# Loading gate and up weights from two DMA queues, and half of a filter from the Pool queue, in a spectral + GEGLU block

## Chip, cores and metric

One core of one Trainium2 chip. The metric is the device time of one execution in microseconds (us); where several executions were timed, the median is given with the lowest and highest. "Span" is the profiled time from the first to the last instruction, some 2 us shorter than the device time.

TensorE is PE, VectorE DVE, ScalarE ACT, GpSimd POOL, SyncE SP. In this kernel PE, DVE and ACT compute (ACT also issues one table load), SP only issues DMAs, and POOL does both.

## The reference, cut to what matters

```python
x = A_x                                     # 2048 x 576, bf16
h = x + irfft2(rfft2(layernorm(x)) * (w_r + 1j * w_i))    # filter w: 2048 x 289, real and imaginary plane
n = layernorm(h)
out = h + (gelu(n @ w_gate) * (n @ w_up)) @ w_down         # w_gate, w_up: 576 x 4608, w_down: 4608 x 576
```

## The kernel before

The kernel has two parts. The spectral part does both FFTs as matmuls with tables: stage A (scaled tables x X), stage D/B (tables, filter multiply on DVE), stage I/N (inverse). The feed-forward part works on four blocks of 512 rows; for each it computes gate and up (K = 576 as 9 slices of 64 rows: gate on the upper 64 rows of the array, up on the lower 64), then the down projection.

A small scheduler (`Prog`) turns read and write keys into semaphore waits. Each engine executes its own list in order; `P.dma(ENGINE, ...)` puts a DMA into that engine's list and so on that engine's queue.

The loads, in the order in which SP issues them (`...` marks cuts):

```python
for i, (c0, c1) in enumerate(((0, 2), (2, 4), (4, 8), (8, 12), (12, 16))):
    P.dma(SP, XO[:, c0:c1, :], xv[:, c0:c1, :], f"x{i}", ...)            # X tiles
P.dma(ACT, ATB..., dram["ATAB"])                                         # the table that is scaled
P.dma(SP, FT ...); P.dma(SP, BT ...); P.dma(SP, VT ...)                  # tables
for hf, (g0, g1) in enumerate(((1, 9), (9, 16))):                        # filter: 36 small DMAs, rows of 578 B
    for pl, src in ((0, A_w_r), (1, A_w_i)):
        ...  P.dma(SP, WS[jj:64:4, g0:g1, pl, 0:K2], a, f"w{pl}{hf}", ...)
P.dma(SP, DT ...); P.dma(SP, IT ...); P.dma(SP, IDT ...)                 # tables of the inverse stage
```

The weights of the feed-forward part. Gate lies on partitions 0 to 63 of `WGU`, up on 64 to 127. `WD` shares its memory with the filter and the spectral data, so w_down must wait until the filter multiply is over (the `alias`):

```python
P.op(POOL, None, r=["IT", "DT"])            # Pool waits until IT and DT have landed
for j in range(9):
    f0, f1 = 512 * j, 512 * j + 512
    P.dma(POOL, WGU[0:64, :, f0:f1], wgv[:, :, f0:f1], f"wg{j}", w=[("WG", j, 0)])
    P.dma(POOL, WGU[64:128, :, f0:f1], wuv[:, :, f0:f1], f"wg{j}", w=[("WG", j, 1)])
P.alias(ukeys + wkeys[0] + wkeys[1] + [...], [("WD", j) for j in range(9)])
for j in range(9):
    P.dma(POOL, WD[:, 4 * j:4 * j + 4, :], wdv[:, 4 * j:4 * j + 4, :], f"wd{j}", w=[("WD", j)])
```

Block 0's activations are turned on PE while the inverse stage runs (tiles c = 0 to 3, at passes 7, 9, 11, 13 of 16), evicted to `HT0`, and then each half is copied to the other half of the partitions by two small SBUF-to-SBUF DMAs on SP's queue. These eight copies ("HT<-HT", 256 rows of 256 B each) are what the first gate/up matmul waits for:

```python
def turn_pe(c):
    ...                                                     # 5 matmuls with the identity, one DVE copy to HT0
    P.dma(SP, HT0[0:64, 5:9, t0:t1], HT0[64:128, 0:4, t0:t1], f"tr{c}", ...)
    P.dma(SP, HT0[64:128, 5:9, t0:t1], HT0[0:64, 1:5, t0:t1], f"tr{c}", ...)
for c in range(NT + 1):                                     # inverse stage
    ...
    if c in (6, 8, 10, 12): norm((c - 6) // 2)
    if c in (7, 9, 11, 13): turn_pe((c - 7) // 2)
```

## Time and profile before

| | before |
|---|---|
| device time, median of 3 | 535.7 us (535.35 to 536.09) |
| span of the profiled run | 534.1 us |
| PE busy | 508.4 us, 95% |
| first spectral matmul (FT,U) | 21.4 us |
| first gate load issued | 35.5 us |
| first gate/up matmul | 106.5 us |

PE at 95% looks like a kernel with nothing left. The chain of waits shows the rest. Its columns are start in us, length in us, and what it was: an engine with the tile and line it worked on, a DMA in flight, or an engine's sequencer ("SPq").

```profile
90.23 16.04 DMA HT_69<-HT_69
106.27 0.25 issue
106.52 4.03 PE PS L683 x18
...
115.38 64.41 PE PS L683 x593
```

One wait of 16 us stands between the spectral part and the feed-forward part, on the HT<-HT copies. After 115 us the chain is PE alone. (HT_69 is `HT0`, L683 the gate/up matmul.)

The DMA table gives, for each kind of DMA, how often, the size of one, and the median time from issue to landing: 16 us for a copy of 64 KB.

```profile
HT_69<-HT_69 SPq DMA_DIRECT2D x8, 64.0 KB, 16.0
```

The stretches of 10 us show why. Columns: stretch, its length, busy us (and instructions) of PE, PEld, DVE, ACT and POOL; then the granted clock, the busy share of the DMA engines, and GB/s.

```profile
core 0: us, PE busy (x) PEld busy (x) DVE busy (x) ACT busy (x) POOL busy (x), PEclk, DMA share, GB/s
0.00:10.00 10.00, 7.19 (x24) 2.71 (x24) 4.09 (x16) 5.24 (x14) 3.52 (x11) 1.00 0.82 312
10.00:20.00 10.00, 9.26 (x86) 6.32 (x87) 8.97 (x40) 9.20 (x23) 2.76 (x3) 0.83 0.91 244
20.00:30.00 10.00, 9.01 (x76) 6.29 (x74) 5.64 (x17) 4.92 (x11) 0.00 (x0) 1.00 0.43 92
30.00:40.00 10.00, 10.00 (x90) 7.19 (x89) 7.60 (x28) 6.18 (x13) 4.55 (x6) 1.00 0.66 195
40.00:50.00 10.00, 10.00 (x90) 7.17 (x88) 7.61 (x29) 6.18 (x13) 8.74 (x13) 1.00 1.03 216
...
90.00:100.00 10.00, 0.46 (x4) 0.15 (x2) 0.77 (x2) 2.00 (x5) 0.00 (x0) 0.69 1.05 339
```

From 40 us on the DMA engines are full (share 1.03), at 216 GB/s with gate and up and 339 GB/s with w_down. Between 20 and 30 us they are less than half busy: there SP issues filter loads one after another, and Pool waits. Pool's timeline (start, length, engine, line, operation, tiles, in brackets the idle time before it and what ended it):

```profile
14.98 1.04 POOL L419 TENSOR_TENSOR ATS<-ATB,RS_56 128x512 bf16<-128x512 bf16 x1 [1.66 <-DVE RS_56 L417]
35.45 0.92 POOL L193 DMA_DIRECT2D WGU<-in_B_w_gate_dram  x1 [19.43 <-DMA IT<-c_itab]
```

### The profile page before, as it was taken

What the parts mean: (1) busy time and instruction counts of PE and PEld (TensorE: products, weight loads), DVE (VectorE), ACT (ScalarE), POOL (GpSimd) and SP (SyncE); (2) the same over time, 40 slices, a digit from 0 to 9 for tenths busy, and PEclk for the clock granted to TensorE, in tenths of its full rate; (3) what the DMA queues carried; (4) which work ended last, traced back from release to release, by engine and by line L of the source; (5) the groups of instructions that cost most, each with busy time, mean ns of one, the idle gap of its engine ahead of it and who ended that gap; (6) DMA issues with size and microseconds to landing.
All of it is one profiled execution on the core that took longest, in us unless ns stands there. A gap on an engine that the chain in (4) does not pass through costs nothing.

```text
span 534.1 us, 10212 instructions
## 1 busy us (share of the span) xinstructions
PE 508.4 (95%) x4427; PEld 296.4 (55%) x4427; DVE 184.2 (34%) x428; ACT 152.8 (29%) x285; POOL 26.3 (5%) x40
## 2 busy tenths in 40 slices
PE   7999897099999999999999999999999999999997
PEld 3667575034444677444446774444477744444776
DVE  5677667033443211344332113433321133333111
ACT  6756587033243100233331002333210033223000
POOL 3036220000000000000000000000000000000000
PEclk9999999589999999999999999999999999999999
DMA  8669999801110000011100000111000000000000
GB/s 326 137 169 215 215 216 270 273 1 26 26 26 17 7 18 18 9 26 28 24 14 6 18 18 12 26 26 26 11 7 18 18 6 1 1 1 2 12 18 18
DMA packets 34684, 30.76 MB, mean 58 GB/s; under 512 B 21296, under 2 KB 29616, under 8 KB 34640
## 3 DMA queue, kind: packets, MB, share of 16 engines
q0 software_dynamic: 4176, 15.93, 12.5%
q1 hardware_dynamic: 30320, 13.66, 9.6%
q8 instruction: 35, 0.57, 0.5%
q10 hardware_dynamic: 144, 0.52, 0.3%
q14 instruction: 9, 0.07, 0.0%
HBM read 23.67 MB, written 2.36 MB: 49 GB/s over the span
## 4 chain that ended last, share of the span: by engine, by line
PE 91%; DMA 4%; DVE 3%; ACT 1%; issue 1%; POOL 0%; SPq 0%; DVEq 0%; POOLq 0%
PE PS L683 52%; PE PS L699 27%; PE PS L513 4%; DMA HT_69<-HT_69 3%; PE PS L590 3%; PE PS L527 1%; PE PS L546 1%; PE PS L435 1%; DMA XO<-in_A_x_dram 1%; PE PS L428 1%; DVE XO L602 1%; PE PS L550 1%; PE PS L599 1%; ACT JNK L392 0%; DVE HT_69 L648 0%
## 5 line engine op out<-in xcount | busy, mean ns | idle before, releaser
L690 ACT ACTIVATE GL<-PS 128x512 bf16<-128x512 f32 x144 | 85.8, 597 | 294.1 <-PE PS L683 286.7
L683 PE MATMUL PS<-HT_69,WGU 64*128 64x512 bf16 x1296 | 142.8, 380 | 16.2 <-DMA HT_69<-HT_69 16.1
L691 DVE TENSOR_TENSOR AT<-GL,PS 128x512 bf16<-128x512 bf16 x144 | 98.7, 687 | 167.4 <-ACT GL L690 167.2
L699 PE MATMUL PS<-WD,AT 128*128 128x288 bf16 x1152 | 141.8, 286 | 0.0
L683 PE MATMUL PS<-HT_84,WGU 64*128 64x512 bf16 x1296 | 140.2, 376 | 0.0
L699 PEld LDWEIGHTS PS<-WD,AT 128*128 128x128 bf16 x1152 | 112.4, 98 | 29.9 <-issue 1.7
L683 PEld LDWEIGHTS PS<-HT_69,WGU 64*128 64x128 bf16 x1296 | 63.4, 95 | 94.7 <-issue 18.7
L683 PEld LDWEIGHTS PS<-HT_84,WGU 64*128 64x128 bf16 x1296 | 62.9, 94 | 76.8 <-issue 0.5
L702 DVE TENSOR_TENSOR OS<-PS,XO 128x288 bf16<-128x288 f32 x32 | 14.7, 458 | 123.7 <-PE PS L699 123.7
L590 PE MATMUL PS<-DT,V 128*128 128x288 bf16 x160 | 22.1, 286 | 0.5 <-ACT V L553 0.5
L513 PE MATMUL PS<-FT,U 128*128 128x289 bf16 x160 | 22.3, 287 | 0.0
L602 DVE SCALAR_TENSOR_TENSOR XO<-PS,XO 128x576 bf16<-128x576 f32 x16 | 12.1, 757 | 27.9 <-PE PS L599 27.7
L590 PEld LDWEIGHTS PS<-DT,V 128*128 128x128 bf16 x160 | 15.4, 98 | 4.3 <-issue 0.6
L605 ACT ACTIVATE SQ<-XO 128x576 bf16<-128x576 bf16 x16 | 10.9, 683 | 23.2 <-DVE XO L602 23.0
L513 PEld LDWEIGHTS PS<-FT,U 128*128 128x128 bf16 x160 | 14.4, 97 | 5.1 <-issue 0.4
L428 PE MATMUL PS<-ZD 128*128 128x512 bf16 x39 | 12.0, 462 | 1.3 <-POOL ZD L356 1.3
L628 DVE TENSOR_SCALAR HN<-XO,TM,RS_59 128x576 bf16<-128x576 bf16 (+1 forms) x32 | 10.2, 361 | 8.0 <-DMA HT_84<-HN 6.2
L546 PE MATMUL PS<-VT,ZS 128*128 128x256 bf16 x64 | 9.6, 271 | 2.4 <-DVE ZS L537 1.6
L399 DVE BATCH_NORM_STATS2 ST_53<-XO 128x6 f32<-128x288 bf16 x24 | 9.2, 443 | 5.6 <-DMA XO<-in_A_x_dram 5.6
L532 DVE TENSOR_TENSOR T_79<-YS,WS 128x580 bf16<-128x580 bf16 x16 | 7.4, 460 | 10.4 <-ACT YS L530 10.4
L530 ACT ACTIVATE YS<-PS 128x578 bf16<-128x578 f32 x16 | 10.5, 656 | 1.5 <-PE PS L527 0.3
L592 ACT ACTIVATE GS<-PS 128x576 bf16<-128x576 f32 x16 | 10.2, 635 | 2.6 <-PE PS L590 2.6
(57 smaller groups left out, 170.8 us busy)
## 6 DMA issues: line engine op xcount, KB each, us to landing
WGU<-in_B_w_gate_dram POOLq DMA_DIRECT2D x9, 576.0 KB, 22.8
WGU<-in_B_w_up_dram POOLq DMA_DIRECT2D x9, 576.0 KB, 24.8
WD<-in_B_w_down_dram POOLq DMA_DIRECT2D x9, 576.0 KB, 31.6
out_dram<-OS SPq DMA_DIRECT2D x32, 72.0 KB, 1.6
XO<-in_A_x_dram SPq DMA_DIRECT2D x3, 576.0 KB, 6.9
HT_84<-HN SPq DMA_TRANSPOSE x72, 2.4
FT<-c_ftab SPq DMA_DIRECT2D x1, 725.0 KB, 8.9
DT<-c_dtab SPq DMA_DIRECT2D x1, 720.0 KB, 4.6
```

The costliest lines, as they stand in the source:

```text
L428: P.op(PE, lambda t: t.matmul(bank(7), ZD[:, 0:128], ZD[:, :], start=True, stop=True), r=["ZD"], w=[("PS", 7)])
L513: P.op(PE, lambda t, b=b, o=o, dt=dt, g=g: t.matmul(bank(b, 0, 128, 0, K2), U[:, dt, g, :, :], FT[:, dt, o, 0:K2], start=(dt == 0), stop=( ...
L530: P.op(ACT, lambda a, sl=sl: a.activation(YS[:, sl, :, 0:K2], banks(4, 2, K2), ACTF.Copy), r=[("PS", 4), ("PS", 5)], w=[("Y", sl)])
L546: P.op(PE, lambda t, c=c, zp=zp, sl=sl, sp_=sp_: t.matmul(bank(6, 0, 128, 256 * c, 256 * c + 256), ZS[:, sl, zp, 128 * c:128 * c + 128], V ...
L590: P.op(PE, lambda t, b=b, h=h, kt=kt, c=c: t.matmul(bank(b, 0, 128, 0, 288), V[:, kt, c, :, :], DT[:, kt, 288 * h:288 * h + 288], start=(k ...
L602: P.op(DVE, lambda v, x2=x2, c=c: v.scalar_tensor_tensor(x2, banks(4, 2, 288), 1.0, x2, op0=ALU.mult, op1=ALU.add, accum_out=SB2[:, 0, c:c ...
L605: P.op(ACT, lambda a, sl=sl, c=c: a.activation(SQ[:, sl, :], XO[:, c, :], ACTF.Square, accum_out=SB2[:, 1, c:c + 1]), r=[("X", c)], w=[("S ...
L683: P.op(PE, lambda t, o=o, h0=h0, kt=kt, sl=sl, f=f, b0=b0, HT=HT: t.matmul(bank(b0 + o), WGU[h0:h0 + 64, kt, 128 * f:128 * f + 128], HT[h0 ...
L690: P.op(ACT, lambda a, s2=s2, b0=b0: a.activation(GL[:, s2, :], bank(b0), ACTF.Gelu_apprx_tanh), r=[("PS", b0)], w=[("GL", s2)])
L691: P.op(DVE, lambda v, s2=s2, b0=b0, f=f: v.tensor_tensor(AT[:, f, :], GL[:, s2, :], bank(b0 + 1), op=ALU.mult), r=[("GL", s2), ("PS", b0 + ...
L699: P.op(PE, lambda t, b0=b0, h=h, f=f, p=p: t.matmul(bank(b0 + h, 0, 128, 0, 288), AT[:, f, 128 * p:128 * p + 128], WD[:, f, 288 * h:288 * ...
L702: P.op(DVE, lambda v, b0=b0, h=h, p=p, c=c: v.tensor_tensor(OS[:, p % 2, 288 * h:288 * h + 288], bank(b0 + h, 0, 128, 0, 288), XO[:, c, 28 ...
```

## The change

Its intent: start the weights earlier and load gate and up at the same time, so that the copies find free DMA engines. The imaginary filter plane moves from SP to Pool, in the gaps between Pool's table scalings; Pool no longer waits for IT and DT; the up weights go on SP's queue.

```diff
-    for hf, (g0, g1) in enumerate(((1, 9), (9, 16))):
-        for pl, src in ((0, A_w_r), (1, A_w_i)):
-            ... all 36 filter loads on SP
+    def w_loads(pl, hf, eng):
+        ... the same loads, returned as a list of calls that issue on eng
+    for f in w_loads(0, 0, SP) + w_loads(0, 1, SP):      # real plane
+        f()
 ...
+    for f in w_loads(1, 0, POOL):                        # imaginary plane, first half: 8 loads
+        f()
+    wrest = w_loads(1, 1, POOL)                          # second half: 10 loads
 ...
     ln1_scale(0, POOL)
+    for f in wrest[:4]: f()
 ...
     ln1_scale(1, POOL)
+    for f in wrest[4:7]: f()
 ...
     ln1_scale(2, POOL)
+    for f in wrest[7:]: f()
 ...
-    P.op(POOL, None, r=["IT", "DT"])
     for j in range(9):
         f0, f1 = 512 * j, 512 * j + 512
         P.dma(POOL, WGU[0:64, :, f0:f1], wgv[:, :, f0:f1], f"wg{j}", w=[("WG", j, 0)])
-        P.dma(POOL, WGU[64:128, :, f0:f1], wuv[:, :, f0:f1], f"wg{j}", w=[("WG", j, 1)])
+        P.dma(SP, WGU[64:128, :, f0:f1], wuv[:, :, f0:f1], f"wu{j}", w=[("WG", j, 1)])
```

More of the change, by code (lines that the diff above doesn't have):

```diff
@@ L367, in _build @@
     P.dma(SP, VT[:, :, :, :].rearrange("p a b c -> p (a b c)"), dram["VTAB"][:, :], "vt", w=["VT"])
-    for hf, (g0, g1) in enumerate(((1, 9), (9, 16))):
-        for pl, src in ((0, A_w_r), (1, A_w_i)):
-            for jj in range(4):
-                a = bass.AP(src.tensor, (16 * jj + g0) * K2, [[128 * K2, 16], [K2, g1 - g0], [1, K2]])
-                P.dma(SP, WS[jj:64:4, g0:g1, pl, 0:K2], a, f"w{pl}{hf}", r=["Wz"], w=[("W", hf, pl, jj)])
-                a = bass.AP(src.tensor, (64 + 16 * jj + 16 - g0) * K2, [[128 * K2, 16], [-K2, g1 - g0], [1, K2]])
-                P.dma(SP, WS[64 + jj:128:4, g0:g1, pl, 0:K2], a, f"w{pl}{hf}", r=["Wz"], w=[("W", hf, pl, 4 + jj)])
-            if hf:
-                for p0 in range(2):
-                    a = bass.AP(src.tensor, 64 * p0 * K2, [[128 * K2, 16], [16 * K2, 4], [1, K2]])
-                    P.dma(SP, WS[64 * p0:64 * p0 + 64, 0, pl, 0:K2], a, f"w{pl}{hf}", r=["Wz"], w=[("W", hf, pl, 8 + p0)])
+    def w_loads(pl, hf, eng):
+        g0, g1 = ((1, 9), (9, 16))[hf]
+        src = (A_w_r, A_w_i)[pl]
+        o = []
+        for jj in range(4):
+            o.append((WS[jj:64:4, g0:g1, pl, 0:K2], (16 * jj + g0) * K2, [[128 * K2, 16], [K2, g1 - g0], [1, K2]], jj))
+            o.append((WS[64 + jj:128:4, g0:g1, pl, 0:K2], (64 + 16 * jj + 16 - g0) * K2, [[128 * K2, 16], [-K2, g1 - g0], [1, K2]], 4 + jj))
+        if hf:
+            for p0 in range(2):
+                o.append((WS[64 * p0:64 * p0 + 64, 0, pl, 0:K2], 64 * p0 * K2, [[128 * K2, 16], [16 * K2, 4], [1, K2]], 8 + p0))
+        return [lambda d=d, off=off, ap=ap, h=h: P.dma(eng, d, bass.AP(src.tensor, off, ap), f"w{pl}{hf}", r=["Wz"], w=[("W", hf, pl, h)]) for d, off, ap, h in o]
+    for f in w_loads(0, 0, SP) + w_loads(0, 1, SP):
+        f()
     GORD = list(range(1, NG)) + [0]
@@ L459, in _build @@
     ln1_scale(0, POOL)
+    for f in wrest[:4]:
+        f()
     ln1_tile(5)
@@ L471, in _build @@
     ln1_scale(1, POOL)
+    for f in wrest[4:7]:
+        f()
     ln1_tile(9)
@@ L484, in _build @@
     ln1_scale(2, POOL)
+    for f in wrest[7:]:
+        f()
     ln1_tile(13)
```

## The prediction

> **What bounds the kernel now.** The feed-forward matmuls are 79% of the chain of waits and untouched: from 115.4 us to 531.5 us the chain is PE alone. What can move lies before. The chain's largest wait is one piece of 16.0 us (90.2 to 106.3): the small SBUF-to-SBUF copies HT<-HT, the turned activations of the first token block. Similar small transfers take 2.2 to 2.8 us (DMA table) when little else runs. These are slow because weights still stream: in the windows view the DMA engines are at 1.02 to 1.06 from 40 to 100 us, at 215 GB/s while gate and up chunks (64 partitions each) load, at 320 to 340 GB/s for w_down (128 partitions). The first gate load is issued only at 35.5 us: the timeline shows Pool idle for 19.4 us, waiting for IT. In the stall the granted clock falls to 0.5, and the first 18 gate/up matmuls take 4.03 us instead of 1.95.
>
> **What changes.** (a) The IT/DT wait goes. SP issues 18 fewer filter loads (0.64 us each) and reaches the up weights at about 18.6 us; Pool reaches the gate weights at about 21 to 22. Gate and up are 10.6 MB: at the old 215 GB/s they end by about 71 us. w_down cannot start before the filter multiply ends (63.4 before, about 66 after) and needs about 17 us: all ends by 84 to 88 us. The Trainium skill, "SBUF — State Buffer", section "Door 1: The DMA port swizzle", gives 64 partitions 8 of 16 ports, about 218 GB/s; the trace's 215 agrees. Its next section says that two DMAs to the two halves gain only 6%; I don't need more, and expect 220 to 300 GB/s. So the last HT copy, issued at about 92 us, meets empty queues: 2.3 us instead of 16.
>
> (b) The cost: Pool now issues 18 filter loads around the table scalings, which are on the chain (POOL ATS, 9.65 to 10.7). Estimate: 0.73 us each, as Pool's weight loads take in the timeline. Eight from 4.05 us end near 10.0, four and three more follow: the third scaling, ended at 16.0 before, ends at 18.7 to 19.7. The early filter packets also interleave with the X tiles, which now arrive just in time (ACT is not idle before tile 7). The spectral stage, starting at 21.4, should start 2 to 3.5 us later.
>
> **Sum.** First gate/up matmul: now 106.5; after 92.3 + 3 = 95.3, a gain of about 11 us. PE is then idle for some 2 us only, so the clock probably stays at 1.0: another 2 us. Total about 12.7 us: 523 us, range 519.5 to 527.5. Faster by over 2% (under 525.0): 0.70; within 2%: 0.29; slower: 0.01.
>
> **What would show each step.** HT<-HT on the chain under 4 us; first gate load issued at 20 to 23 us; first gate/up matmul at 94 to 97 us; first spectral matmul (FT,U) at 23 to 25 us; Pool's issues between scalings 0.6 to 0.9 us each; at most one 3.4 us stretch of clock 0.5 near 92 to 98 us; the part from 115.4 us to the end as long as before.
>
> **What would make it wrong.** Pool's issues cost over 1 us, so the spectral stage slips by 5 us or more (527 to 529); X tiles are starved by filter packets; the up loads, in 1 KB packets against Pool's 4 KB, finish so late that they hold up the HT copies behind them; or the short idle still drops the clock (+2 us). If Pool's issues are cheaper (0.4 us), the result is near 520.

## The result, and the profile after

| | before | after |
|---|---|---|
| device time, median | 535.89 us (535.35 to 537.4, 4 runs) | 528.5 us (526.48 to 529.1, 4 runs) |
| span of the profiled run | 534.1 us | 526.9 us |
| first spectral matmul (FT,U) | 21.37 us | 21.61 us |
| first gate load issued | 35.5 us | 17.9 us |
| last HT<-HT copy landed | 106.3 us | 98.45 us |
| first gate/up matmul | 106.52 us | 98.81 us |
| from there to the end of the span | 427.6 us | 428.1 us |

The ratio is 0.9851, 95% interval 0.9818 to 0.9884. (A ratio is the mean time of one kernel's fast runs over that of the other's of the same rounds, so not quite the ratio of the medians.) The change gains 1.5%, less than the 2% that counts as a verdict, and 528.5 lies above the predicted range.

The chain of waits after:

```profile
88.71 0.74 DVE HT_69 L659
...
91.31 2.04 SPq L193
...
94.94 3.51 DMA HT_69<-HT_69
98.45 0.35 issue
98.81 4.02 PE PS L694 x18
```

The DMA piece shrank from 16.0 to 3.5 us, but that isn't the whole wait. The last tile's DVE copy ended at 89.2 us before and 89.45 us after, and its second HT<-HT copy, which was issued at 90.2 us before, is issued at 94.94 us now. SP could not issue it sooner. The wait has moved in part from "DMA" to "SPq". The DMA table agrees: issue to landing of a copy is now 7.4 us, not 16.0.

```profile
HT_69<-HT_69 SPq DMA_DIRECT2D x8, 64.0 KB, 7.4
```

SP's own timeline suggests that its queue was full (inferred from the times to issue; the trace has no fill level). The nine up loads took SP 51 us to issue, the eight copies 17.8 us (by themselves about 0.6 us each):

```profile
21.27 51.13 SPq L193 DMA_DIRECT2D WGU<-in_B_w_up_dram  x9
78.49 17.82 SPq L193 DMA_DIRECT2D HT_69<-HT_69  x8
```

The stretches of 10 us after (four left out, with 200 to 304 GB/s and a share of 1.05 to 1.13; columns as before):

```profile
0.00:10.00 10.00, 7.43 (x24) 2.77 (x24) 4.20 (x16) 4.53 (x11) 7.88 (x19) 1.00 0.83 292
10.00:20.00 10.00, 7.79 (x81) 4.96 (x83) 8.72 (x39) 9.66 (x25) 9.97 (x16) 1.00 1.07 267
20.00:30.00 10.00, 8.81 (x77) 6.29 (x76) 5.88 (x18) 4.99 (x11) 4.49 (x7) 1.00 1.10 221
30.00:40.00 10.00, 10.00 (x90) 7.19 (x88) 7.35 (x28) 6.18 (x13) 0.00 (x0) 1.00 1.03 209
...
80.00:90.00 10.00, 9.91 (x88) 7.48 (x86) 8.91 (x27) 8.27 (x20) 0.00 (x0) 1.00 1.05 318
90.00:100.00 10.00, 1.89 (x12) 0.78 (x12) 0.98 (x5) 2.09 (x5) 0.00 (x0) 0.72 0.79 155
```

The DMA engines are now busy from 10 us until the copies have landed (a share of 1.03 to 1.13 up to 90 us, 0.93 from there to 98.45 us). The column GB/s times 10 us can be added up. Up to 20 us 5.6 MB have moved in both kernels (before 312 + 244, after 292 + 267). Up to the first gate/up matmul 24.3 MB move in both. So after 20 us 18.7 MB are still to come, whoever issues them. The change filled the idle of the stretch 20 to 40 us; it removed no bytes.

Which queue got what comes from the DMA records of the trace, here for 72 to 88 us after the change. A packet is one such record. The means include the records of a few bytes that end a DMA:

| queue | packets | mean size | mean time of one | rate |
|---|---|---|---|---|
| Pool's (w_down) | 992 | 4.1 KB | 211 ns | 254 GB/s |
| SP's (the last up loads) | 993 | 1.0 KB | 56 ns | 62 GB/s |

The packet counts are equal: the queues take turns, packet by packet. Pool's packets hold four rows (4.1 KB of gate, 4.6 KB of w_down), SP's a single row. The rows of gate and up are equally long (1 KB each), so the difference is how the rows went into packets on the two queues. The filter shows it too: its rows of 578 B went in packets of one row on SP's queue and of up to eight rows (4.6 KB) on Pool's. The Trainium skill, "DMA: Bandwidth & Descriptors", section "Queues, rings and completion order", says that each DMA engine goes round between its queues packet by packet, and the counts 992 and 993 agree. With turns of 4 to 1 KB, the up loads crawl at 62 GB/s while w_down streams. The last two up chunks landed at 94.4 and 96.8 us, and the copies stood behind them in SP's queue.

Pool's side of the change went better than I had expected:

```profile
3.94 4.31 POOL L193 DMA_DIRECT2D WS<-in_A_w_i_dram  x8
9.55 1.03 POOL L425 TENSOR_TENSOR ATS<-ATB,RS_56 128x512 bf16<-128x512 bf16 x1 [1.30 <-issue]
10.53 2.16 POOL L193 DMA_DIRECT2D WS<-in_A_w_i_dram  x4
...
15.33 1.05 POOL L425 TENSOR_TENSOR ATS<-ATB,RS_56 128x512 bf16<-128x512 bf16 x1
17.91 6.59 POOL L193 DMA_DIRECT2D WGU<-in_B_w_gate_dram  x9
```

A filter load (128 rows) takes Pool 0.54 us to issue (4.31 / 8), not the 0.73 us of a weight load (576 rows; 6.59 / 9). The issues mostly fit between the scalings, the third of which starts 0.35 us later than before. The spectral stage starts 0.24 us later.

### The profile page after: what moved, and what is told of

Its sections match the earlier page's. It is cut to its first block, busy times and chain, and to the rows that moved or that the text cites. A ratio compares the mean times of both kernels' runs of the same rounds, so it can differ in the third digit from the quotient of the medians.

```text
span 526.9 us, 10210 instructions
## 1 busy us (share of the span) xinstructions
PE 507.8 (96%) x4425; PEld 302.5 (57%) x4427; DVE 184.1 (35%) x428; ACT 152.8 (29%) x285; POOL 29.1 (6%) x49
## 4 chain that ended last, share of the span: by engine, by line
PE 88%; SPq 3%; DVE 3%; DMA 3%; ACT 2%; issue 1%; DVEq 0%; ACTq 0%
PE PS L694 51%; PE PS L710 27%; PE PS L525 4%; PE PS L601 3%; SPq L191 2%; DMA XO<-in_A_x_dram 2%; PE PS L539 1%; SPq L193 1%; PE PS L558 1%; ACT U L453 1%; DMA HT_69<-HT_69 1%; PE PS L610 1%; PE PS L562 1%; DVE XO L613 1%; DMA HT_84<-HN 0%
## 5 line engine op out<-in xcount | busy, mean ns | idle before, releaser
L694 PEld LDWEIGHTS PS<-HT_69,WGU 64*128 64x128 bf16 x1296 | 70.8, 95 | 79.8 <-issue 11.7
L694 PEld LDWEIGHTS PS<-HT_84,WGU 64*128 64x128 bf16 x1296 | 62.6, 94 | 77.1 <-issue 0.5
L434 PE MATMUL PS<-ZD 128*128 128x512 bf16 x37 | 10.9, 447 | 1.5 <-POOL ZD L356 1.3
```

The source lines that it names most:

```text
L434: P.op(PE, lambda t: t.matmul(bank(7), ZD[:, 0:128], ZD[:, :], start=True, stop=True), r=["ZD"], w=[("PS", 7)])
L694: P.op(PE, lambda t, o=o, h0=h0, kt=kt, sl=sl, f=f, b0=b0, HT=HT: t.matmul(bank(b0 + o), WGU[h0:h0 + 64, kt, 128 * f:128 * f + 128], HT[h0 ...
```

## The experiments

Theory A: the feed-forward part starts when the HT<-HT copies land, and these land when the bulk streams get out of their way. In the changed kernel they stand behind the last up loads in SP's queue, and those crawl because w_down takes 4 KB turns. Rivals: B, the copies or their issue by SP are slow in themselves; C, what counts is how early the loads start; D, standing in one queue is the whole cause, and sharing the engines is harmless.

e1 to e4 ran on one chip with 7 runs of the kernel before (median 535.88), e5 to e8 on another (535.77, 7 runs), e9 to e11 on a third (535.57, 9 runs). Each has its own profile. In all of them the output was correct.

| run | base | edit | time us (lowest to highest) | ratio to before (95%) | first gate/up matmul us |
|---|---|---|---|---|---|
| e1 | after | w_down after the copies | 520.75 (520.42 to 523.1) | 0.9725 (0.9702 to 0.9749) | 92.97 |
| e2 | before | w_down after the copies | 520.14 (520.04 to 521.43) | 0.9710 (0.9695 to 0.9725) | 92.43 |
| e3 | after | copies on ACT's queue | 528.12 (526.68 to 528.75) | 0.9848 (0.9827 to 0.9869) | 98.98 |
| e4 | after | up in rows of 3 KB | 522.65 (522.27 to 523.96) | 0.9756 (0.9739 to 0.9772) | 94.79 |
| e5 | after | up back on Pool's queue | 528.58 (526.52 to 529.73) | 0.9847 (0.9812 to 0.9881) | 100.05 |
| e6 | before | up on SP, no IT/DT wait; filter stays on SP | 527.43 (526.69 to 529.68) | 0.9836 (0.9802 to 0.9871) | 101.23 |
| e7 | before | e2 + turns up to two passes earlier | 520.0 (518.47 to 521.16) | 0.9689 (0.9658 to 0.9720) | 90.91 |
| e8 | after | e1 + e4 | 521.13 (520.23 to 521.45) | 0.9709 (0.9678 to 0.9741) | 92.95 |
| e9 | before | e2 again | 520.37 (519.51 to 522.15) | 0.9718 (0.9699 to 0.9736) | 92.07 |
| e10 | after | e1 + turns up to two passes earlier | 521.77 (520.44 to 523.27) | 0.9734 (0.9720 to 0.9749) | 94.04 |
| e11 | before | e7 again | 520.08 (519.36 to 521.16) | 0.9710 (0.9695 to 0.9724) | 91.05 |

### e1: the changed kernel, w_down issued after the copies

w_down is first read at about 172 us in the changed kernel, so it needn't hurry. It must not be in flight when the copies are:

```diff
-    for j in range(9):          # where it stood, ahead of the inverse stage
-        P.dma(POOL, WD[:, 4 * j:4 * j + 4, :], ...)
 ...                             # after the inverse stage's loop:
+    P.op(POOL, None, r=[("HT", 0, i, k) for i in range(4) for k in (1, 2)])
+    for j in range(9):
+        P.dma(POOL, WD[:, 4 * j:4 * j + 4, :], ...)
```

> The changed kernel, but the w_down loads are issued only after the four pairs of HT<-HT copies have landed (w_down is first read at about 172 us). Theory A (the copies wait in SP's own queue behind the last up chunks, which crawl at 62 GB/s because w_down takes the engines in 4 KB packets at 255 GB/s): the up loads run alone at 200 GB/s from 64 us and end near 80 us, the last copy lands near 92 us, first gate/up matmul at 92 to 93 us instead of 98.8, clock stays near 1.0, time 520 to 522 us. Rival B (the copies, or SP's issue of them at 0.8 to 4.2 us each, are slow whatever else streams): start stays at 97 to 99 us, time 527 to 529 us.

Measured 520.75 us, first gate/up matmul at 92.97 us. With w_down out of the way the last up chunk landed at 79.9 us (96.8 in the changed kernel), and SP issued each copy in about 0.6 us. The chain:

```profile
90.46 2.16 DMA HT<-HT
...
92.97 2.12 PE PS L695 x18
```

And the line of the DMA table, median 2.1 us from issue to landing (7.4 in the changed kernel):

```profile
HT<-HT SPq DMA_DIRECT2D x8, 64.0 KB, 2.1
```

Theory A holds, B falls: from DVE's last copy to the landing of the same copies, issued by the same engine, it takes 2.8 us (89.81 to 92.62) instead of 9.0 (89.46 to 98.45). The first 18 matmuls take 2.12 us instead of 4.02, as the clock stayed at 1.0 (PE stood still only for some 2 us). The span falls by 8.3 us: 5.84 of them are the earlier start, the other 2.5 come after it. The edit frees the up loads as well as the copies, so it does not tell standing in SP's queue from sharing the engines; e3 and e5 do.

### e2: the kernel before, w_down issued after the copies

The same edit on the kernel before, with nothing of the change.

> The kernel before, with nothing of the change, but w_down issued after the HT<-HT copies. Theory A: gate and up still end near 89 us, the copies then meet empty engines, first gate/up matmul at 92 to 94 us instead of 106.5, time 520 to 523 us: as good as or better than the change. Rival C (what counts is that the loads start early, as the change does): the stall shrinks little, first matmul later than 98 us, time 527 us or more.

Measured 520.14 us: 2.9% under the kernel before, and as good as e1.

```profile
90.06 2.12 DMA HT<-HT
...
92.43 2.12 PE PS L684 x18
```

Here the gate and up loads start at 35 us as before and land by 87.6 us; the copies are done by 92.2 us. Rival C falls: the early start isn't needed. Of the 16.0 us of that wait before, 2.1 remain: 13.9 were lost to w_down streaming during the copies. And the change as a whole is worth nothing once w_down is late (e1 is no faster than e2).

### e3: the changed kernel, copies on ACT's queue

```diff
-    P.dma(SP, HT0[0:64, 5:9, t0:t1], ...)
-    P.dma(SP, HT0[64:128, 5:9, t0:t1], ...)
+    P.dma(ACT, HT0[0:64, 5:9, t0:t1], ...)
+    P.dma(ACT, HT0[64:128, 5:9, t0:t1], ...)
```

> The changed kernel with the eight HT<-HT copies issued by ACT, so on a queue of their own, not behind the up loads. If standing in line behind the up loads on one queue is the whole cause: first gate/up matmul at 92 to 94 us, time 521 to 524 us (ACT loses some 0.6 us per issue). If the sharing of the engines by turns is what counts (one 256 B copy packet for each 4 KB w_down packet and 1 KB up packet, some 270 ns a turn): the copies end only when the streams end, at 96 to 98 us, time 527 to 531 us.

Measured 528.12 us, first gate/up matmul at 98.98 us: no gain from a queue of one's own.

```profile
94.11 4.51 DMA HT<-HT
...
98.98 3.81 PE PS L694 x18
```

```profile
HT<-HT ACTq DMA_DIRECT2D x8, 64.0 KB, 9.8
```

The DMA records of 86 to 92 us show three queues in turn: 350 packets of w_down, 349 of up, 350 of the copies (0.24 KB), while w_down moved 243 GB/s and the copies 14. A copy has 256 rows, one packet each; spread evenly over 16 engines, it needs 16 turns. Rival D falls as the whole cause. The verdict has a flaw: the issues also delayed ACT, so the last copy was issued at 94.1 us instead of 90.1, and PE waited for ACT in the inverse stage. By then w_down was nearly over. That the copies would have been slow at 90 us too rests on the packet counts, on the first pair (issued at 80.1 and 80.8 us, while both streams ran, it landed only at 91.6 and 96.1) and on e5.

### e4: the changed kernel, up weights in rows of 3 KB

```diff
-        P.dma(SP, WGU[64:128, :, f0:f1], wuv[:, :, f0:f1], f"wu{j}", w=[("WG", j, 1)])
+        if j % 3 == 0:
+            f1 = f0 + 1536
+            P.dma(SP, WGU[64:128, :, f0:f1], wuv[:, :, f0:f1], f"wu{j}", w=[("WG", j + i, 1) for i in range(3)])
```

> The changed kernel with the up loads in 3 DMAs of 1536 columns (3 KB rows) instead of 9 of 512 (1 KB rows), so that gate and up take turns of nearly equal size. Theory A with the port theory ([...]side by side fails because turns are 4 KB to 1 KB): both stream together at 300 GB/s or more in all (254 now), both end before 68 us, w_down ends near 84 us, first gate/up matmul at 92 to 93 us, time 520 to 522 us. If two DMAs to the two halves can't run side by side (rate stays at 215 to 255 GB/s): the loads end at 90 us or later, first matmul at 94 to 98 us, time 523 to 528 us.

Measured 522.65 us, first gate/up matmul at 94.79 us: between the two cases. Where both streams run, the rate is 305 GB/s, and falls to 209 GB/s when up is alone:

```profile
42.00:56.00 14.00, 14.00 (x124) 10.06 (x121) 10.83 (x41) 8.44 (x17) 0.00 (x0) 1.00 1.03 305
60.00:68.00 8.00, 6.01 (x53) 3.96 (x52) 4.13 (x17) 4.05 (x7) 3.91 (x6) 1.00 1.03 209
```

So gate and up can be loaded side by side, at 305 GB/s against 215 for one half of the partitions (before, 40 to 84 us), if their turns are of like size (3.7 and 2.9 KB in the records of 44 to 54 us). With 1 KB packets on SP's queue the same phase of the changed kernel reached 256 GB/s (202 + 54, 48 to 54 us; 247 over the longer stretch 44 to 56 us). My expectation that both would end before 68 us was wrong: SP's queue first carries filter, DT and IT, so up was beside gate only from about 40 to 57 us, and the last up load landed at 81.1 us. w_down then landed at 93.2 us, still among the copies.

### e5: the changed kernel, up back on Pool's queue

```diff
-        P.dma(SP, WGU[64:128, :, f0:f1], wuv[:, :, f0:f1], f"wu{j}", w=[("WG", j, 1)])
+        P.dma(POOL, WGU[64:128, :, f0:f1], wuv[:, :, f0:f1], f"wg{j}", w=[("WG", j, 1)])
```

> The changed kernel with the up loads back on Pool's queue: filter plane on Pool and the early start stay, the splitting over two queues goes. If the weights' total of bytes at 215 to 220 GB/s for half the partitions is what sets the end of the loads: gate and up end near 78 us, w_down (4 KB packets) streams to about 95 us, and the copies, no longer behind up loads but taking turns with w_down, land at 96 to 98 us: first gate/up matmul 96 to 98.5, time 525 to 528.5 us, so the splitting is worth nothing or costs a little. If the splitting is what helped: later than 100 us, time 530 us or more.

Measured 528.58 us, first gate/up matmul at 100.05 us, about 1.5 us past the expected range, the time at its edge.

```profile
90.01 9.79 DMA HT<-HT
...
100.05 3.64 PE PS L694 x18
```

```profile
HT<-HT SPq DMA_DIRECT2D x8, 64.0 KB, 12.6
```

This closes the gap that e3 left. The copies have SP's queue to themselves, the last is issued at 90.01 us, and it still takes 9.8 us, because w_down streams until 99.0 us. The records of 86 to 94 us: 625 packets of w_down (320 GB/s), 626 of the copies (19 GB/s). It also shows that the splitting over two queues is worth nothing in time here: without it the kernel has the same time as with it (528.5).

### e6: the filter plane left on SP

The kernel before, without the IT/DT wait and with up on SP's queue; Pool loads no filter.

```diff
-    P.op(POOL, None, r=["IT", "DT"])
 ...
-        P.dma(POOL, WGU[64:128, :, f0:f1], ..., f"wg{j}", w=[("WG", j, 1)])
+        P.dma(SP, WGU[64:128, :, f0:f1], ..., f"wu{j}", w=[("WG", j, 1)])
```

> The kernel before with the IT/DT wait removed and up on SP's queue, but both filter planes left on SP. Theory A: gate loads then start at about 16 us and take turns of 4 KB against 578 B with the filter loads, so the second filter half lands at 45 to 50 us, just when it is needed (45 us), DT and IT after it; spectral stage late by 0 to 4 us, the up loads on SP start later still and end later: first gate/up matmul 98 to 103 us, time 528 to 534 us. If moving the filter plane is of no use: same as the change, 528 to 529 us.

Measured 527.43 us, just under the expected range (the profiled execution 529.68, inside it), first gate/up matmul at 101.23 us. The spectral stage now waits for the filter, as the list of waits of the stretch 40 to 62 us shows (who waited, for what; us in total, times, longest):

```profile
DVE T L532 <- DMA WS<-in_A_w_i_dram: 6.4, 1, 6.4
```

The gate packets of 4 KB hold up the 578 B filter rows on SP's queue: from 25 to 43 us the records show 886 packets of gate at 183 GB/s and 879 of SP's queue at 25 GB/s. So the filter's move to Pool has a use: without it the multiply stalls 6.4 us. Yet the time comes out as that of the changed kernel within the scatter. In this profile w_down landed at 99.5 us and the last copy at 100.9, so the end of all loads, and not the late spectral stage alone, sets the start of the feed-forward part here too.

### e7 and e8: towards a better version

e7 is e2 with the turns of block 0 earlier, so that the copies land before PE ends the inverse stage:

```diff
-        if c in (6, 8, 10, 12): norm((c - 6) // 2)
-        if c in (7, 9, 11, 13): turn_pe((c - 7) // 2)
+        if c in (6, 7, 9, 10): norm((6, 7, 9, 10).index(c))
+        if c in (7, 8, 10, 11): turn_pe((7, 8, 10, 11).index(c))
```

> The kernel before with w_down late (as in e2), and the turning of the four tiles of block 0 moved two passes earlier in the inverse stage (tile 3 turned at pass 11 instead of 13). The last copy lands at about 89 us, before PE ends its stage at 90 us, so the wait of some 2 us is gone: first gate/up matmul at 90 to 91 us, time 517.5 to 519 us. If the earlier turns only crowd VectorE, PE's stage ends later by as much and the time stays at 520 us.

Measured 520.0 us. The first gate/up matmul moved as expected, to 90.91 us with no wait for the copies, and the profiled execution took 518.47 us; the other three took 519.85 to 521.16. The median lies above the expected 517.5 to 519 us: a miss, taken up in e11.

e8 joins e1 and e4.

> The changed kernel with both repairs, up loads in 3 KB rows and w_down late. Gate and up end near 72 us or sooner instead of 80, but the copies land at 92.5 us as in e1: the time stays at 520 to 521.5 us, that of e1 and e2. If it is faster than e1 by 1 us or more, the loads still mattered.

Measured 521.13 us, first gate/up matmul at 92.95 us. The loads are now done at 74.9 us and the DMA engines are mostly idle until 93 us (share 0.13), and it brings nothing: with w_down late, the loads are not waited for.

### e9, e10, e11: e2, e1 and e7 more closely

e9 is the kernel of e2, e11 that of e7, e10 is e1 with the turns of e7.

> The kernel of e2 again, on the same chip and in the same rounds as the next two, with more rounds: 520.1 us within 1 us.

> The changed kernel with w_down late and the turns of block 0 two passes earlier. If the change is worth something of its own once the order is mended, it beats the next run by 0.5 us or more; I expect 518.5 to 520 us, no better than the next run, since the spectral stage starts 0.2 to 0.5 us later with the change and the loads are no longer waited for.

> The kernel of e7 again with more rounds, to tell whether the earlier turns are worth the 2 us by which the first gate/up matmul moved (92.4 to 90.9 us in the profiles): 518 to 519 us, 1 to 2 us under e2 in the same rounds, if they are; the same as e2 within 0.5 us if not.

Measured 520.37 (e9, as expected), 521.77 (e10, expected 518.5 to 520) and 520.08 us (e11, expected 518 to 519 or the same as e2; it is the same). e11 is not told apart from e9: the earlier turns are worth less than the scatter. In e11 the first gate/up matmul comes 1.0 us earlier than in e9, but PE waits further on. The chain of e11 passes through block 1's turning, which runs as 36 DMA transposes on SP's queue, about 1.23 us each; DVE's next normalization waits for the buffer that they read, and the multiply behind it in DVE's list comes late:

```profile
126.78 2.37 DMA HT<-HN
...
129.81 0.60 DVE AT L692
```

PE is idle for 1.4 us of the 20 us from 120 to 140 us in this profile, and not at all in e7's profiled execution (518.47 us). But e9's profile has the same idle, 0.8 us long, so it takes back some 0.6 us of the 1.0 us gained. What takes the rest, and what makes the scatter of some 2 us, isn't shown.

e10 is slower than e11 by 1.7 us in the median. In its profiled execution (523.27 us) the clock was 0.5 from 63.8 to 70.6 us: around the end of the filter multiply PE has little to do (busy 8.0 of the 10 us from 60 to 70 us, in e11 too), and here the first inverse passes ran at half clock:

```profile
65.67 4.96 PE PS L598 x20
```

The same group takes 2.61 us in e11. Without those 2.35 us this execution would be at about 521. For the other four only the mean clock is known, 0.997 as in e11's. What keeps e10 above e11 there stays open. That it is no better than e11 was expected; its time lies above the expected range.

## Why the prediction was wrong, point by point

- **"What bounds the kernel now": right.** The copies were held up by the streaming weights (e1, e2).
- **"(a) ... at the old 215 GB/s they end by about 71 us ... all ends by 84 to 88 us": this step failed.** w_down ended at 95.2 us and up at 96.8 us. What was mis-sized is the bytes: I counted 10.6 + 5.3 = 15.9 MB from about 20 us, where 18.7 MB were to come: DT, IT and IDT (1.3 MB), the copies (0.5 MB) and the rest of the filter were in the queues too, and had been spread over idle DMA time before. At the measured 243 GB/s (18.7 MB in the 77 us from 20 to 97 us) the missing 2.8 MB are 11.5 us: 84 to 88 becomes 95 to 99. The rate was about right: 15.9 MB from 21.5 us to 84 or 88 would be 254 or 239 GB/s. The order also differed, as the last up chunks crawl in 1 KB turns beside w_down's 4 KB, but that decided which stream ended last and not when the loads ended: in e5, with up on Pool's queue, they ended at 99.0 us.
- **"So the last HT copy ... meets empty queues: 2.3 us instead of 16": wrong for that reason.** From DVE's last copy to landing it took 9.0 us (89.46 to 98.45). My list of what could go wrong had it ("finish so late that they hold up the HT copies"), without weight in the sum.
- **"(b) the spectral stage ... 2 to 3.5 us later": wrong, in the other direction.** 0.24 us. Pool's filter loads cost 0.54 us to issue instead of 0.73, and mostly fit into Pool's gaps. X tiles did come late (ACT waited 0.93 us for one at 10.1 us), and it was absorbed.
- **"The clock probably stays at 1.0: another 2 us": wrong in the changed kernel** (0.5 from 94.3 to 104.5 us, first 18 matmuls 4.02 us), right where the copies land in time (2.12 us in e1 and e2). So from the first gate/up matmul to the end it took as long as before (428.1 and 427.6 us), and the 2 us were not gained.
- **"first gate/up matmul at 94 to 97 us":** 98.81. The sum closes: 98.81 instead of 95.3 is 3.5 us, the clock 2 us; 523 + 5.5 = 528.5, the measured time. That it closes to a tenth is partly luck, as the runs scatter by 2.6 us.
- **"HT<-HT on the chain under 4 us": met to the letter (3.51), and no sign of success:** the rest of the wait stood under SP's sequencer.
- **"220 to 300 GB/s" for gate and up together: about right** (247 to 256), and 305 with packets of like size (e4). The section that the prediction calls the next one is "Can I just issue two DMAs to hit both halves?", two sections on.
- **First gate load at 20 to 23 us, FT,U at 23 to 25 us:** 17.9 and 21.6, both earlier, by the cheaper issues.

The change's 7 us come mostly from starting the loads in DMA time that was idle: from 20 to 40 us 4.3 MB moved instead of 2.9, and at 243 GB/s the 1.4 MB are some 5.9 us, an estimate, of the 7.7 us by which the start moved. The rest isn't accounted for. Splitting the loads over two queues added nothing measurable (e5).

## What to carry to other kernels

Before speeding up a load, ask who needs it and when: one load issued 100 us before its use cost this kernel 15 to 16 us (e2, e9), by standing in the way of small copies that were needed at once. Add up all bytes that are queued, not only those that are moved, and if the DMA engines are full from then on, an earlier start gains only the idle time that it fills. Between queues that share the engines by turns, the size of a packet sets the share: small packets lose to large ones. And look at how rows become packets: here rows of 1 KB went four to a packet on Pool's queue and one to a packet on SP's, so of two equal weights the one on SP's queue crawled.

## What the Trainium skill lacked or had wrong

- "SBUF — State Buffer", section "Can I just issue two DMAs to hit both halves?", says no: two DMAs to the two halves gain 6%; "DMA: Bandwidth & Descriptors", "Rules for kernel authors", calls it not worth the bother. Here gate (partitions 0 to 63) and up (64 to 127) on two queues reached 247 to 256 GB/s with turns of 4 and 1 KB and 305 GB/s with turns of near equal size, against 215 for one half: 15% to 19% and 42% more. The 215 for one half agrees with the 218 of the SBUF page, section "Door 1: The DMA port swizzle".
- The same DMA page has the round between queues by packet, with 9 to 17 descriptors as typical for one. Here, if a record of the trace is the page's packet, one of the copies, the filter or up on SP's or ACT's queue was a single row (0.26, 0.58, 1.0 or 3.1 KB), and one on Pool's queue held four rows of the weights (4.1 to 4.6 KB) or up to eight of the filter (4.6 KB). What follows isn't on the page: at equal counts of packets (992 and 993) the rates were 254 and 62 GB/s, and a 64 KB copy took 9.8 us beside a 320 GB/s stream and 2.1 us without it.
- The same page, section "Issuing engines are not separate DMA queues", calls the time to issue usually small beside the DMA. It was not while the engines were full: SP needed 51.1 us for nine up loads, and the last copy behind them was issued 4.7 us later than before (94.94 instead of 90.23).
- No page that I used has Pool's time to issue by size: 0.54 us for a load of 128 rows, 0.73 us for 576 rows (means of 8 and 9 loads).
- "TensorE: Matmul & The Clock Gate", "Part 1: The HAM clock gate", has a free-running window of 3413 ns. The trace agrees: within the kernels, the stretches at 0.5 lasted 3.41, 6.83, 10.24 or 17.07 us. For a kernel's start the page says that the same kernel meets a different number of slow matmuls from run to run; the runs show such chance in mid-kernel. In the 12 profiles other than e6, PE never stood still for over 0.8 us from 60 to 64 us; the clock fell to 0.5 then or within 1 us of it in e10 (for 6.83 us) and e3 (for 3.41 us), and in none of the ten others. What sets these two apart isn't shown.
